# Thresholded attention and a bilinear feed-forward on one core: the key slot shared by two heads is spread over four tiles of the array, and a part of it is added by VectorE

## The chip, the cores and the metric

The kernel runs on one core of a Trainium2 chip. The metric is the device time of one execution in microseconds. Before the change it was 1560.83 us in the median of three runs (1559.9 to 1564.76). One further execution was profiled; it took 1561.63 us, and its instructions span 1559.9 us.

In what follows TensorE is PE in the profile, VectorE is DVE, ScalarE is ACT, GpSimd is POOL, and SyncE, which issues most DMAs, is SP.

## The reference

There are 8 batches, 8 heads, 576 positions and a head dimension of 64. All values are float32.

```python
scores = scale * q @ k.T
thresh = max(scores, axis=-1) - tau
attn = exp(where(scores >= thresh, scores, -1e9) - max)
attn = attn / (sum(attn) + 1e-9)
x = (attn @ v)                 # heads side by side: (4608, 512)
out = ((x @ w_a) * (x @ w_b)) @ w_out      # d_ff = 1536
```

The change touches the line `attn @ v` alone.

## The kernel before, in words

**Pairs and units.** Two heads of a batch form a pair, so there are 32 pairs, four to a batch. A pair's 576 queries are cut into five units: four of 128 queries for each of both heads, and a last one with the 64 remaining queries of both heads. The main loop runs over 160 units, `g` counting them. In the first batch the units are ordered for an early start. From the second batch on, units 0 and 1 of all four pairs of a batch come first, and then units 2, 3 and the last one pair by pair.

**What a unit does.** `scores` (L303) writes the scores of 128 rows into one PSUM tile per head, and the last unit into a single one; the last unit uses only the two tiles on the diagonal of the array. VectorE takes the maxima (`mx`, L319), GpSimd scales them (L320), ScalarE takes the exponential (L332), and VectorE masks by the threshold and sums (`w`, L336). ScalarE normalises (L355). In the next iteration `turn_blocks` (L393) transposes blocks on VectorE and writes them to a scratch in DRAM, from where `turn_back` reads them as `wT`, with keys on the partitions. The first eight units go through TensorE instead. Queries and keys of later pairs are transposed by VectorE too (`prep`, L282, tiles `qT` and `kT`), two and one iterations ahead of their first use.

**The product.** `weighted` (L483) runs three iterations after the last unit of its part, at the end of the iteration but for a fifth of the feed-forward's share. It has 256 query columns, or 320 where the 64 tail queries ride along; in the first batch the tails are products of 64 columns, and the first eight units are products of 128 in `weighted_unit` (L469). `product` (L441) uses the array as four tiles of 64 by 64. A tile (r, j) reads the 64 partitions of half r and writes those of half j. The 576 keys of two heads fill nine slots of 128 partitions: head 0 has slots 0 to 3, head 1 has slots 5 to 8, and slot 4 (`NT`) holds 64 keys of head 0 in its lower half and 64 keys of head 1 in its upper half. So in slots other than 4 all four tiles work, two on each head, and in slot 4 only tiles (0, 0) and (1, 1). The two halves of the key rows of a head go into two banks, `pv[:, 0]` and `pv[:, 1]`, and `join` (L437) adds them: ScalarE copies the first into `xT` and VectorE adds the second. For 320 columns a second `join` does the same for the tail, into `xt`.

**The feed-forward** works in blocks of 256 tokens. Its matmuls (`pab` and `po`, L530 and L550) are a generator that `advance` steps by as many columns as the iteration is owed. When the four pairs of a block are done, GpSimd copies `xT` with its partition halves exchanged into `xS` (L459), and the block is queued.

**What sets the order.** The order of the instructions on every engine is the order in which the program writes them; `keep_order` ties each to the one before. All PSUM tiles come from one pool of four buffers of two banks each: scores, `pab`, `po` and `pv` take turns, and a matmul that opens a tile waits until the last reader of an earlier one is done. `make_room` (L596) moves the feed-forward into the middle of a `pab` or `po` before a product takes its tile.

Of the kernel before, what the change touches and what calls it, by code (L numbers as in the profile page):

```python
# [14 lines left out]
ALU = mybir.AluOpType  # L15
# [35 lines left out]
def kernel(  # L51
# [36 lines left out]
    nc = tc.nc  # L88
    B, H, S, D = q.shape
    P = 128  # L90
    Q = 32
# [3 lines left out]
    NT = 4  # L95
    MAIN = NT * P
    TAIL = S - MAIN
# [7 lines left out]
    GT = HALF // TAIL  # L105
# [16 lines left out]
    def banks(n, name):  # L122

        return psum.tile([P, 2, 512], FP32, tag="banks", name=name)[:, :, 0:n]
# [43 lines left out]
    for f in range(NG):  # L168
        for c in range(HP):
            for dst, w in ((wa_sb, w_a), (wb_sb, w_b)):  # L170
                src = []
                for r in range(2):
                    chunks = [(2 * c + e) % HP * 2 + (r + (c >= HP // 2)) % 2 for e in range(2)]
                    cols = slice(f * CW + r * CH, f * CW + (r + 1) * CH)
                    rows = w[:, cols].bitcast(U32).rearrange("(k p) f -> p k f", p=D)
# [69 lines left out]
    for _ in range(2):  # L245
        t = work.tile([P, 2 * NB, 2 * Q], FP32, tag="tb", bufs=2, name="rows")
        t = t.rearrange("p n e -> p (n e)")[0:R]
# [11 lines left out]
    for name in ("q", "k"):  # L259
        t = work.tile([P, CW, 2], FP32, tag="xT", bufs=XT_BUFS, name="rows")  # L260
        t = t.rearrange("p n e -> p (n e)")[0:R, 0:2 * NR * D]
# [17 lines left out]
    x_of, xtail_of = {}, {}  # L279
# [110 lines left out]
    def width(i, h):  # L390
        return (HALF, HALF, TAIL)[h] if i < HP else (HALF, HALF + TAIL)[h]
# [45 lines left out]
    def join(out, lo, hi):  # L437
        nc.scalar.copy(out, lo)  # L438
        nc.vector.tensor_tensor(out, out, hi, op=ALU.add)  # L439

    def product(wT, vm, n):  # L441

        pv = banks(n, "pv")
        for s in (NT, 0, 1, 2, 3):
            for r in range(2):
                rows = slice(r * D, (r + 1) * D)
                for j in ((r,) if s == NT else range(2)):
                    k0 = NT if s == NT else 5 * j + s
                    nc.tensor.matmul(pv[j * D:(j + 1) * D, r], vm[rows, k0], wT[rows, k0],  # L449
                                     start=(s == (NT if j == r else 0)), stop=(s == NT - 1))  # L450
        return pv

    def x_tile(name):
        return work.tile([P, HP, HALF], FP32, tag="xT", bufs=XT_BUFS, name=name)
# [14 lines left out]
    def weighted_unit(i, u):  # L469

        b, hp = pairs[i]
        pv = product(turned.pop((i, u, "pe")), loaded[i]["v"], P)
        if (b, 0) not in x_of:
            x_of[b, 0] = x_tile("xT")
            state["xs"] = x_tile("xS")
        join(x_of[b, 0][:, hp, u * P:(u + 1) * P], pv[:, 0], pv[:, 1])
        exchange(x_of[b, 0], state["xs"], hp, u * P, (u + 1) * P, nc.vector)
        if hp == HP - 1:
            state["rows"] = u + 1
            if u == 0:  # L480
                blocks.append(((x_of[b, 0], state["xs"]), ("first", b, 0)))

    def weighted(i, h):  # L483

        b, hp = pairs[i]
        n = width(i, h)
        pv = product(turned.pop((i, h)), loaded[i]["v"], n)
        if h < 2:
            if hp == 0:
                x_of[b, h] = x_tile("xT")  # L490
            lo, hi = (pv[:, r, 0:HALF].rearrange("p (i t e) -> p i t e", t=2, e=Q) for r in range(2))
            join(x_of[b, h][:, hp, :].rearrange("p (t i e) -> p i t e", t=2, e=Q), lo, hi)
            if hp == HP - 1:
                complete.append((x_of.pop((b, h)), ("half", b, h)))
        if n % HALF:
            t = b % GT
            if hp == 0 and t == 0:
                xtail_of[b // GT] = x_tile("xt")
            join(xtail_of[b // GT][:, hp, t * TAIL:(t + 1) * TAIL], pv[:, 0, n - TAIL:n], pv[:, 1, n - TAIL:n])
            del loaded[i], prepared[i]  # L500
            if hp == HP - 1 and t == GT - 1:
                complete.append((xtail_of.pop(b // GT), ("tail", b - t, 0)))
# [120 lines left out]
    n = 0  # L623
# [8 lines left out]
    for g in range(len(units) + PV_LAG):  # L632
# [5 lines left out]
        if here:  # L638
            i, u = units[g]
# [60 lines left out]
        n = g - PV_LAG  # L700
        if BY_PE <= n < len(units) and part(*units[n]):
            make_room()
            weighted(*part(*units[n]))
            running["owed"] -= (NSLOT + 1) // 2 * width(*part(*units[n]))
# [38 lines left out]
```

## Time and profile before

| | |
|---|---|
| median of three runs | 1560.83 us |
| profiled execution | 1561.63 us, span 1559.9 us |
| mean granted TensorE clock | 0.985 |
| TensorE, matmuls | 1490.9 us busy, 22640 records |
| VectorE | 881.9 us, 1844 |
| ScalarE | 592.7 us, 935 |
| GpSimd | 260.3 us, 662 |
| HBM | 127.40 MB read, 89.65 MB written |

A group line gives the source line, the engine, the operation, out<-in by tile names, the shapes and the count; then the busy time in us and the mean of one in ns; then the idle time of the engine just before such instructions and what ended most of it. A line of the timeline gives start in us, length in us, engine, source line, operation and count. A line of the chain gives start, length and what it was. A window line gives, after the stretch and its length, busy us of PE, weight loads, DVE, ACT and POOL with counts, then the granted clock, the share of the DMA engines and GB/s. A float32 matmul leaves two records, one for each of its two passes.

### The profile page before, as it was taken

To read this page: it belongs to the slowest core of one execution; us is meant where nothing else is said; L and a number is where in the kernel's file an instruction comes from. 1 tells how busy PE (TensorE), PEld (TensorE's weight loads), DVE (VectorE), ACT (ScalarE), POOL (GpSimd) and SP (SyncE) were. 2 spreads that over 40 slices of the span, in tenths; PEclk is the share of its full clock that TensorE was granted. 3 is DMA by queue.
4 is the path that set the end of the run, shared out by engine and by line. 5 is a ranking of instruction groups with operands and counts; after the bars stand their busy time and mean duration, and the time that the engine had idled before them with its cause. 6 is when DMAs were issued, how large, how long until landed. Compare 5 with 4: busy or idle time off the path is not lost.

```text
span 1559.9 us, 51105 instructions
## 1 busy us (share of the span) xinstructions
PE 1490.9 (96%) x22640; PEld 1087.8 (70%) x22640; DVE 881.9 (57%) x1844; ACT 592.7 (38%) x935; POOL 260.3 (17%) x662
## 2 busy tenths in 40 slices
PE   5779999898999999999999999999999999999998
PEld 3666585674768777677867686867686768586775
DVE  5999576465656665675544755466555765510010
ACT  4767344343434443443332443243433443310000
POOL 2666211111111111121100101011110111010000
PEclk8889999998999999999999999999999999999999
DMA  9648887679767886687455965588657976530000
GB/s 202 147 139 225 179 159 166 141 151 193 158 141 169 175 194 142 157 171 179 101 128 117 187 151 140 114 174 180 150 130 140 186 160 140 130 85 16 2 15 15
DMA packets 624558, 220.38 MB, mean 141 GB/s; under 512 B 542929, under 2 KB 612049, under 8 KB 624337
## 3 DMA queue, kind: packets, MB, share of 16 engines
q1 hardware_dynamic: 621968, 216.52, 63.4%
q8 instruction: 178, 2.92, 0.8%
q10 hardware_dynamic: 2368, 0.59, 0.2%
q14 instruction: 44, 0.35, 0.1%
HBM read 127.40 MB, written 89.65 MB: 139 GB/s over the span
## 4 chain that ended last, share of the span: by engine, by line
PE 77%; DVE 8%; DMA 5%; SPq 3%; ACT 2%; issue 2%; POOL 0%; DVEq 0%; POOLq 0%; ACTq 0%
PE pab L530 42%; PE po L550 19%; PE pv L449 8%; PE sc L312 8%; SPq L411 2%; DVE w L336 2%; DMA wT<-swap 2%; DVE mx L319 2%; DMA swap<-tb 2%; DVE low L226 1%; DVE tb L401 1%; SPq L140 1%; DMA qm<-in_q_dram 1%; SPq L423 0%; DMA raw<-in_moe_w_b_dram 0%
## 5 line engine op out<-in xcount | busy, mean ns | idle before, releaser
L550 PE MATMUL po<-wo_sb,h 64*64 64x512 f32 x3456 | 410.1, 590 | 0.0
L332 ACT ACTIVATE w<-sc,bias,scalars 128x576 f32<-128x576 f32 x288 | 228.6, 829 | 237.1 <-POOL bias L320 233.8
L550 PEld LDWEIGHTS po<-wo_sb,h 64*64 64x64 f32 x3456 | 178.8, 133 | 178.9 <-issue 166.5
L319 DVE TENSOR_REDUCE mx<-sc 128x1 f32<-128x576 f32 x288 | 205.8, 751 | 163.8 <-PE sc L312 160.1
L355 ACT ACTIVATE w<-w,rcp 128x576 f32<-128x576 f32 x272 | 197.7, 769 | 234.5 <-DVE rcp L349 234.5
L320 POOL TENSOR_SCALAR bias<-mx,scalars 128x1 f32<-128x1 f32 x288 | 84.8, 294 | 1073.5 <-DVE mx L319 1042.9
L530 PE MATMUL pab<-xS,wa_sb 64*64 64x256 f32 (+1 forms) x3520 | 260.2, 377 | 2.4 <-POOL xS L459 2.4
L312 PE MATMUL sc<-kT,qT 64*64 64x288 f32 x2304 | 239.6, 412 | 21.4 <-DVE kT L301 8.1
L530 PE MATMUL pab<-xS,wb_sb 64*64 64x256 f32 (+1 forms) x3520 | 257.3, 375 | 0.0
L336 DVE SCALAR_TENSOR_TENSOR w<-sc,thr,w 128x576 f32<-128x576 f32 x288 | 222.6, 805 | 18.0 <-ACT w L332 13.8
L530 PE MATMUL pab<-xT,wb_sb 64*64 64x256 f32 (+1 forms) x3136 | 224.2, 378 | 3.2 <-DVE h L538 1.6
L530 PE MATMUL pab<-xT,wa_sb 64*64 64x256 f32 (+1 forms) x3136 | 221.8, 373 | 4.9 <-DVE xT L439 3.5
L530 PEld LDWEIGHTS pab<-xS,wa_sb 64*64 64x64 f32 x3520 | 182.2, 134 | 34.9 <-POOL xS L459 9.0
L530 PEld LDWEIGHTS pab<-xS,wb_sb 64*64 64x64 f32 x3520 | 183.7, 134 | 27.2 <-issue 0.3
L449 PE MATMUL pv<-wT,vm 64*64 64x320 f32 (+3 forms) x2592 | 180.4, 389 | 13.9 <-DMA wT<-swap 13.2
L312 PEld LDWEIGHTS sc<-kT,qT 64*64 64x64 f32 x2304 | 137.5, 134 | 71.7 <-issue 26.2
L530 PEld LDWEIGHTS pab<-xT,wa_sb 64*64 64x64 f32 x3136 | 158.6, 133 | 33.0 <-DVE xT L439 3.8
L530 PEld LDWEIGHTS pab<-xT,wb_sb 64*64 64x64 f32 x3136 | 160.4, 136 | 30.4 <-DVE h L538 2.6
L449 PEld LDWEIGHTS pv<-wT,vm 64*64 64x64 f32 x2592 | 129.8, 136 | 59.9 <-issue 24.5
L401 DVE STREAM_TRANSPOSE tb<-w 128x576 f32<-128x576 f32 x240 | 171.2, 751 | 0.0
L538 DVE TENSOR_TENSOR h<-h,pab 128x512 f32<-128x512 f32 (+1 forms) x110 | 72.6, 660 | 139.3 <-PE pab L530 135.7
L439 DVE TENSOR_TENSOR xT<-xT,pv 128x256 f32<-128x256 f32 (+1 forms) x68 | 27.5, 404 | 208.2 <-ACT xT L438 208.2
(59 smaller groups left out, 769.5 us busy)
## 6 DMA issues: line engine op xcount, KB each, us to landing
swap<-tb SPq DMA_DIRECT2D x240, 288.0 KB, 5.1
wT<-swap SPq DMA_DIRECT2D x28, 1440.0 KB, 7.6
wT<-swap SPq DMA_DIRECT2D x32, 1152.0 KB, 6.2
vm<-in_v_dram SPq DMA_DIRECT2D x32, 288.0 KB, 4.2
swap<-tbt SPq DMA_DIRECT2D x128, 72.0 KB, 2.5
out_dram<-osb SPq DMA_DIRECT2D x32, 256.0 KB, 3.8
qm<-in_q_dram SPq DMA_DIRECT2D x112, 72.0 KB, 3.5
km<-in_k_dram SPq DMA_DIRECT2D x112, 72.0 KB, 4.8
```

Of the source, the lines that this page charges most:

```text
L312: nc.tensor.matmul(sc[j if u < NT else 0][to, c], qT[r, q0:q0 + D], kT[r, c * SH:(c + 1) * SH], start=True, stop=True)
L319: nc.vector.tensor_reduce(mx[:, c], sc[j], axis=AX.XY, op=ALU.max)
L320: nc.gpsimd.tensor_scalar(bias[:, c], mx[:, c], e_nscale, None, op0=ALU.mult)
L332: nc.scalar.activation(w.rearrange("p (c k) -> p c k", c=2), s, AF.Exp, bias=bias[:, j:j + 1], scale=e_scale)
L336: nc.vector.scalar_tensor_tensor(out=wv, in0=s, scalar=thr[:, j:j + 1], in1=wv, op0=ALU.is_ge, op1=ALU.mult, accum_out=sums[:, j:j + 1])
L355: nc.scalar.activation(w, w, AF.Copy, scale=rcp[:, j:j + 1])
L401: nc.vector.transpose(tb[:, j * NB:(j + 1) * NB, (u % 2) * Q:(u % 2 + 1) * Q], w.rearrange("p (n e) -> p n e", e=Q))
L411: nc.sync.dma_start(swap[:, :, g * 2 * Q:(g + 1) * 2 * Q].rearrange("c p w -> p c w"), tb[g * Q:(g + 1) * Q])
L449: nc.tensor.matmul(pv[j * D:(j + 1) * D, r], vm[rows, k0], wT[rows, k0], start=(s == (NT if j == r else 0)), stop=(s == NT - 1))
L530: nc.tensor.matmul(pab[c * D:(c + 1) * D, r], w[rows, f // n, k, fs + c * D:fs + (c + 1) * D], moving, start=(k == 0), stop=(k == H - 1))
L538: nc.vector.tensor_tensor(ht, ht, pab, op=ALU.mult)
L550: nc.tensor.matmul(po[c * D:(c + 1) * D, r], ht[rows, t0:t0 + D], wo_sb[rows, F, :], start=(F == 0), stop=(F == NF - 1))
```

## The change

In `product` slot 4 comes last instead of first. Its diagonal tiles compute only the first 128 columns (`m`). The other columns, 128 of 256 or 192 of 320, are computed by the two tiles off the diagonal, from the same keys and weights, into further columns `n` to `2 n - m` of the same banks. There they stand in the other partition half than the one they belong to. So after each `join` VectorE adds them to `xT`, 64 partitions at a time, in two adds of 128 columns that read the one half and write the other, and for 320 columns in two more of 64 columns to `xt`. Products of 64 and of 128 columns have no such rest; in them only the order changes.

```diff
     def product(wT, vm, n):
-        pv = banks(n, "pv")
-        for s in (NT, 0, 1, 2, 3):
+        m = min(n, P)
+        pv = banks(2 * n - m, "pv")
+        for s in (0, 1, 2, 3, NT):
             for r in range(2):
                 rows = slice(r * D, (r + 1) * D)
-                for j in ((r,) if s == NT else range(2)):
-                    k0 = NT if s == NT else 5 * j + s
-                    nc.tensor.matmul(pv[j * D:(j + 1) * D, r], vm[rows, k0], wT[rows, k0],
-                                     start=(s == (NT if j == r else 0)), stop=(s == NT - 1))
+                for j in range(2):
+                    cols = slice(j * D, (j + 1) * D)
+                    if s < NT:
+                        nc.tensor.matmul(pv[cols, r, 0:n], vm[rows, 5 * j + s], wT[rows, 5 * j + s],
+                                         start=(s == 0), stop=(s == NT - 1 and j != r))
+                    elif j == r:
+                        nc.tensor.matmul(pv[cols, r, 0:m], vm[rows, NT], wT[rows, NT, 0:m],
+                                         start=False, stop=True)
+                    elif n > m:
+                        nc.tensor.matmul(pv[cols, r, n:2 * n - m], vm[rows, NT], wT[rows, NT, m:n],
+                                         start=True, stop=True)
...
-            join(x_of[b, h][:, hp, :].rearrange("p (t i e) -> p i t e", t=2, e=Q), lo, hi)
+            x = x_of[b, h][:, hp, :].rearrange("p (t i e) -> p i t e", t=2, e=Q)
+            join(x, lo, hi)
+            for r in range(2):
+                to, of = (slice(c * D, (c + 1) * D) for c in (r, 1 - r))
+                more = pv[of, r, n:n + P].rearrange("p (i t e) -> p i t e", t=2, e=Q)
+                nc.vector.tensor_tensor(x[to, 2:4], x[to, 2:4], more, op=ALU.add)
...
-            join(xtail_of[b // GT][:, hp, t * TAIL:(t + 1) * TAIL], pv[:, 0, n - TAIL:n], pv[:, 1, n - TAIL:n])
+            x = xtail_of[b // GT][:, hp, t * TAIL:(t + 1) * TAIL]
+            join(x, pv[:, 0, n - TAIL:n], pv[:, 1, n - TAIL:n])
+            for r in range(2 if n > TAIL else 0):
+                to, of = (slice(c * D, (c + 1) * D) for c in (r, 1 - r))
+                nc.vector.tensor_tensor(x[to], x[to], pv[of, r, n + P:n + P + TAIL], op=ALU.add)
```

## The prediction

> **What bounds the kernel now.** I read the page first, then the granted clock, then one window over the steady part, then the groups with shapes kept apart, and last the timeline and the chain around single products. The page and the window:
>
> ```profile
> span 1559.9 us, 51105 instructions
> PE 1490.9 (96%) x22640; PEld 1087.8 (70%) x22640; DVE 881.9 (57%) x1844; ACT 592.7 (38%) x935; POOL 260.3 (17%) x662
> ...
> 390.00:1400.00 1010.00, 1003.99 (x15408) 744.97 (x15404) 593.54 (x1280) 390.32 (x588) 134.78 (x436) 1.00 0.69 151
> ```
>
> TensorE is busy for 1004.0 of 1010.0 us at full clock there, VectorE (third figure) for 59%. So the time is TensorE's, and VectorE seems to have room. Whether it has room at the place of the change is another question. The groups concerned:
>
> ```profile
> L449 PE MATMUL pv<-wT,vm 64*64 64x320 f32 x1008 | 85.7, 442 | 6.4 <-DMA wT<-swap 6.4
> L449 PE MATMUL pv<-wT,vm 64*64 64x256 f32 x1152 | 78.2, 385 | 6.9 <-DMA wT<-swap 6.8
> L439 DVE TENSOR_TENSOR xT<-xT,pv 128x256 f32<-128x256 f32 x60 | 25.3, 421 | 207.8 <-ACT xT L438 207.8
> L439 DVE TENSOR_TENSOR xt<-xt,pv 128x64 f32<-128x64 f32 x32 | 7.1, 221 | 18.7 <-ACT xt L438 18.7
> L439 DVE TENSOR_TENSOR xT<-xT,pv 128x128 f32<-128x128 f32 x8 | 2.2, 273 | 0.3 <-ACT xT L438 0.3
> ```
>
> A product has 18 matmuls and each leaves two records, so 1152/36 = 32 products have 256 columns and 1008/36 = 28 have 320. One of 256 on TensorE's timeline:
>
> ```profile
> 709.00 2.15 PE L449 MATMUL pv<-wT,vm 64*64 64x256 f32 x34
> 710.79 0.41 PE L312 MATMUL sc<-kT,qT 64*64 64x288 f32 x2
> 710.95 0.42 PE L449 MATMUL pv<-wT,vm 64*64 64x256 f32 x2
> ```
>
> The scores start at 710.79 on the tiles that the shared slot leaves idle, while the product still runs on the other two until 711.16. So the idle tiles are not idle for long, they run ahead; the two tiles on the diagonal set the pace, with ten passes in 2.16 us: 216 ns for 256 columns, 0.844 ns a column (the 320-column passes lie 270 ns apart, the 128-column ones 108).
>
> What follows a product, on the chain that ended last:
>
> ```profile
> 693.14 0.38 ACT xT L438
> 693.54 0.43 DVE xT L439
> 694.00 0.22 ACT xt L438
> 694.25 0.07 DVE xt L439
> 694.38 1.41 DVE mx L319 x2
> 695.80 0.71 DVE tb L401 x2
> 697.77 0.82 DVE w L336 x3
> 698.59 0.69 DVE kT L286
> 699.43 0.42 PE sc L312
> ```
>
> For 6.3 us the end of the kernel hangs on ScalarE and VectorE in order, and TensorE's next scores wait for kT. The change inserts VectorE work in the middle of this.
>
> [...] the two mx reductions overlap by 0.08 us, while the half-partition copies to the other half (L459 on VectorE, first phase) start 0.034 us after the add they need, follow each other 0.014 us apart, and the next instruction comes 0.032 us later. [...] the trace has 273 for 128 and 221 for 64, on 128 partitions, and I use these.
>
> **The change, part by part.** *Removed on TensorE.* A diagonal tile's slot pass shrinks to 128 columns, twice per product: (256-128) x 2 x 0.844 = 216 ns, and (320-128) x 2 x 0.844 = 324 ns. The other two tiles of a 320 product get 192 columns each, 108 ns more than the diagonal; I cost this at nothing because the half-idle last score unit (diagonal only) just before it puts them about 0.4 us ahead. Without that cover it is 28 x 0.108 = 3.0 us. Sum: 32 x 0.216 + 28 x 0.324 = 6.9 + 9.1 = **16.0 us**. Moving the slot from first to last place costs the diagonal nothing; products of 64 and 128 columns change in order only. No DMA is added or moved.
>
> *Added on VectorE.* 32 x 2 + 28 x 4 = 176 adds, about 45 us of busy time. As busy time it would be free. As delay, D: after the join, 0.034 + 0.273 + 0.014 + 0.273 = 0.59 us[...]. For 256 columns mx waits 0.13 us for its scores anyway, so D is 0.49. For 320, ScalarE's copy of xt today waits for VectorE's join of xT (0.03 us after it), so I take it to wait for the two adds too; then the join of xt, two more adds (0.034 + 0.221 + 0.014 + 0.221 = 0.49), and mx, which overlapped by 0.08, is held 0.03: D = 0.59 + 0.49 + 0.11 = 1.2. Bounds for D(320): 0.9 if the copy of xt does not wait for the adds, 1.5 if the adds take the 344 ns that the half-partition copies average. Queued behind on VectorE are both mx, the transposes, the masking with sums (w), and kT; behind ScalarE's xt copy, the next exponentials.
>
> *Who waits.* TensorE's next scores or pab need the PSUM banks that w or the pv joins free, or kT. I took, after each product, the start of the waiting matmul less the end of its VectorE release, less the 0.15 us that such a release takes at least; this is the spare. VectorE's idle time comes only after these waits, so nothing else absorbs D. A matmul may wait with no idle time shown, since a tile still runs: at 653.19 the second score bank waits for w, ended 653.04, while the page counts no gap.
>
> 28 products of 320 columns, by the end of their join: no spare at 310.8, 334.2, 515.7, 538.6, 649.4, 672.8, 694.5, 885.3, 1037.4, 1060.7, 1207.6, 1229.7 (five wait for kT, seven for w); part at 355.8 (0.88), 469.9 (0.66), 492.8 (0.27), 804.7, 834.5, 1155.1, 1323.2 (0.76 each), 860.8 (0.54), 1351.2 (0.46); above 1.2 at the other seven. Loss: 12 x 1.2 = 14.4, plus the nine shortfalls to 1.2, 5.0 us.
> 32 products of 256: no spare at 141.5 (w, and mx does not wait: 0.6), 235.7, 400.8 and 553.8 (kT, 0.49 each): 2.1. Three whole blocks (187, 284, 383 us) start when GpSimd has exchanged x, and it starts after the adds: 3 x 0.59 = 1.8.
> Four or five products start when wT lands (182, 277, 374, 566): a faster product before them gains nothing, about 1.0.
>
> **Sum.** -16.0 + 14.4 + 5.0 + 2.1 + 1.8 + 1.0 = **+8.3 us**. The profiled execution took 1561.63 us with a span of 1559.9; I expect a span near 1568, and against the median of 1560.83 a time of **1569**.
>
> **Rivals.** *Adds hidden (faster).* VectorE is 41% idle in the steady part and idles 3 to 5 us ahead of most joins. Then only the 1 us at the DMAs is lost: -15, 1546. Against it: the chain above, where no TensorE work lies between the joins and the scores.
> *Only waits with visible idle time count (faster to same).* If TensorE makes up the waits that show no gap, because other tiles run on, then kT (5 x 1.2 + 2 x 0.49 = 7.0), the blocks (1.8) and the DMAs (1.0) are left: -6, 1555. For it: full tiles are busy at most of the w waits. Against: the matmuls are issued in order, and at 653.19 all three other tiles start together, late.
> *Slower evacuation than priced.* D(320) of 1.5 and D(256) of 0.8: 12 x 0.3 + 9 x 0.3 + 7 x 0.3 = 8 more, and the lost lead on the narrow tiles 3 more: +19, 1580. It decides once an add exceeds some 0.34 us.
> *It does not do what it says*, the diagonal keeping its pace because the shorter passes are bound by weight loads (133 ns each against 108 of streaming): the early 128-column products do run at 108 ns a pass, so I give it almost nothing; it would be 16 us worse, 1585.
>
> **From cases to numbers.** Mine 0.5 (its own range 1562 to 1577), adds hidden 0.12, visible waits only 0.2, slower adds 0.15, no gain 0.03. What a measurement here can tell from no change is 0.3%, 4.7 us: below 1556.1 is faster, above 1565.5 slower. Adds hidden and half of the visible case are faster: 0.22. The other half and a fifth of mine are the same: 0.2. The rest is slower: 0.58. The range 1552 to 1581 leaves out the hidden case below and a few of the worst above.
>
> **What would show it.** Right: 128-column forms of pv on all four tiles, products of 1.94 and about 2.4 us instead of 2.16 and 2.70 on the diagonal; VectorE busy 925 to 930 us; the adds near 0.27 and 0.22 us; ScalarE's xt copy waiting about 1.1 us for VectorE instead of 0.49; more time in TensorE's waits for kT and w, 1.5 to 2.7 us at the five kT places; the chain with more VectorE than 8%. Wrong: kT and w waits as long as before (adds hidden), adds much over 0.3 us, or the pv passes unchanged in spacing.

## The result, and the profile after

The changed kernel takes **1575.13 us** in the median (1572.78 to 1577.66), the kernel before 1561.64 us in the runs beside it (1559.9 to 1564.76). The medians differ by 13.5 us. The ratio is 1.0084, with a 95% interval of 1.0059 to 1.011: slower by 9 to 17 us, 13.1 in the middle. The profiled execution took 1576.81 us and spans 1575.0. The prediction said 1569, in a range of 1552 to 1581, with a chance of 0.58 on slower.

The page of the changed kernel (the span, the busy times, the chain by engine), and the same steady stretch that was shown of before:

```profile
span 1575.0 us, 51790 instructions
PE 1487.7 (94%) x22880; PEld 1109.0 (70%) x22880; DVE 935.6 (59%) x2020; ACT 592.0 (38%) x935; POOL 261.4 (17%) x662
PE 75%; DVE 11%; SPq 5%; DMA 4%; ACT 2%; issue 2%; POOL 0%; DVEq 0%; POOLq 0%; ACTq 0%
...
390.00:1400.00 1010.00, 990.91 (x15406) 756.29 (x15402) 640.35 (x1429) 391.98 (x589) 135.46 (x437) 1.00 0.70 152
```

TensorE, the first figure of the window, was busy for 1004.0 of these 1010 us and is busy for 990.9 now. It has less to do and waits longer. VectorE has gone from 593.5 to 640.4 us there, and its share of the chain from 8% to 11%. By busy time nothing is full: VectorE stands at 63% of this stretch.

The groups of the changed kernel with shapes kept apart (L458 is the diagonal of slot 4, L461 the two other tiles, L509 and L520 the adds):

```profile
L458 PE MATMUL pv<-wT,vm 64*64 64x128 f32 x272 | 34.7, 276 | 0.0
L461 PE MATMUL pv<-wT,vm 64*64 64x192 f32 x112 | 14.2, 329 | 0.0
L509 DVE TENSOR_TENSOR xT<-xT,pv 64x128 f32<-64x128 f32 x120 | 34.4, 287 | 2.9
L520 DVE TENSOR_TENSOR xt<-xt,pv 64x64 f32<-64x64 f32 x56 | 12.3, 220 | 1.3
```

The shared slot is spread as meant: the tiles off the diagonal take 192 columns in the products of 320 (56 matmuls of two records each), and the diagonal 128. The adds cost 287 and 220 ns, 46.7 us in all. VectorE's busy time grows by 53.7 us on the page. Added up one by one, its instructions take 48.6 us more (980.7 before, 1029.3 after); the other 5.1 us are overlap between neighbours that is gone, such as that of the join of `xt` with the first maxima (0.08 us at 649 us before, where now 0.03 us pass between the last add and the maxima).

A product of 256 columns on the changed kernel's timeline:

```profile
744.18 1.94 PE L455 MATMUL pv<-wT,vm 64*64 64x256 f32 x32
...
746.07 0.27 PE L458 MATMUL pv<-wT,vm 64*64 64x128 f32 x1
746.13 1.18 PE L312 MATMUL sc<-kT,qT 64*64 64x288 f32 x16
```

From its first start to its last end it takes 746.34 - 744.18 = 2.16 us; the one shown of before took 711.37 - 709.00 = 2.37. (The prediction counted ten passes at their pace, 2.16 before and 1.94 after, and so had the product of before end at 711.16.) The 0.21 us are there. The scores now start 0.2 us before the product's end instead of 0.6: the two idle tiles, which had run ahead into them, no longer do.

What follows a product of 320, on the changed kernel's chain, at a place like the one shown of before:

```profile
1072.47 0.38 ACT xT L438
...
1073.33 0.29 DVE xT L509
...
1073.63 0.29 DVE xT L509
...
1073.95 0.22 ACT xt L438
...
1074.93 1.42 DVE mx L319 x2
...
1079.27 0.70 DVE kT L286
...
1080.10 1.72 PE sc L312 x16
```

From the copy to the maxima it was 694.38 - 693.14 = 1.24 us; now it is 1074.93 - 1072.47 = 2.46. So one product of 320 puts VectorE **1.22 us** later. ScalarE's copy of `xt` starts 0.03 us after the second add ends. The next scores still wait for `kT` at the end of it all.

TensorE's waits between 390 and 1420 us (what it waited for, then us in total, times, longest us), before:

```profile
PE sc L312 <- DVE sums L347: 4.4, 5, 1.5
PE pv L449 <- DMA wT<-swap: 1.0, 3, 0.6
PE sc L312 <- DVE kT L286: 0.6, 1, 0.6
```

and the longest after:

```profile
PE sc L312 <- DVE kT L286: 12.7, 6, 2.9
PE sc L312 <- DVE w L336: 2.7, 5, 0.7
PE pab L551 <- POOL xS L471: 2.4, 1, 2.4
```

The waits that the first list puts down to `sums` are waits for `kT`, which VectorE finishes just before (on the chain shown of before, 0.06 us of `sums` come between `kT` and the scores, in a piece not shown). The same six waits for `kT` grow from 5.0 to 12.7 us, by 1.28 in the mean, and waits for `w` appear, with one of 0.6 under `sums` in a line not shown. The wait for the exchanged `xS` is not new: it stands at 393 us, and in the kernel before at 383, just outside this stretch, with 1.2 us.

### The profile page after: what moved, and what is told of

Same layout as the page of the kernel before. It is cut to its first block, busy times and chain, and to the rows that moved or that the text cites. A ratio compares the mean times of both kernels' runs of the same rounds, so it can differ in the third digit from the quotient of the medians.

```text
span 1575.0 us, 51790 instructions
## 1 busy us (share of the span) xinstructions
PE 1487.7 (94%) x22880; PEld 1109.0 (70%) x22880; DVE 935.6 (59%) x2020; ACT 592.0 (38%) x935; POOL 261.4 (17%) x662
## 4 chain that ended last, share of the span: by engine, by line
PE 75%; DVE 11%; SPq 5%; DMA 4%; ACT 2%; issue 2%; POOL 0%; DVEq 0%; POOLq 0%; ACTq 0%
PE pab L551 39%; PE po L571 20%; PE sc L312 8%; PE pv L455 6%; DVE mx L319 3%; SPq L411 2%; DVE w L336 2%; DVE tb L401 2%; DVE low L226 1%; DMA swap<-tb 1%; SPq L140 1%; DMA qm<-in_q_dram 1%; SPq L423 1%; PE pv L458 1%; DMA km<-in_k_dram 0%
## 5 line engine op out<-in xcount | busy, mean ns | idle before, releaser
L571 PE MATMUL po<-wo_sb,h 64*64 64x512 f32 x3456 | 400.8, 590 | 0.1
L571 PEld LDWEIGHTS po<-wo_sb,h 64*64 64x64 f32 x3456 | 192.9, 133 | 161.0 <-issue 131.6
L312 PE MATMUL sc<-kT,qT 64*64 64x288 f32 x2304 | 222.5, 417 | 33.6 <-DVE kT L286 12.7
L551 PE MATMUL pab<-xS,wa_sb 64*64 64x256 f32 (+1 forms) x3520 | 246.4, 376 | 4.7 <-POOL xS L471 4.7
L551 PE MATMUL pab<-xS,wb_sb 64*64 64x256 f32 (+1 forms) x3520 | 244.1, 375 | 0.0
L336 DVE SCALAR_TENSOR_TENSOR w<-sc,thr,w 128x576 f32<-128x576 f32 x288 | 222.6, 805 | 15.8 <-ACT w L332 13.5
L551 PE MATMUL pab<-xT,wa_sb 64*64 64x256 f32 (+1 forms) x3136 | 214.6, 376 | 4.4 <-DVE xT L439 1.8
L551 PE MATMUL pab<-xT,wb_sb 64*64 64x256 f32 (+1 forms) x3136 | 214.8, 376 | 3.4 <-ACT h L557 1.7
L312 PEld LDWEIGHTS sc<-kT,qT 64*64 64x64 f32 x2304 | 125.6, 136 | 84.1 <-issue 45.8
L455 PE MATMUL pv<-wT,vm 64*64 64x256 f32 (+3 forms) x2304 | 163.8, 391 | 15.5 <-DMA wT<-swap 9.3
L455 PEld LDWEIGHTS pv<-wT,vm 64*64 64x64 f32 x2304 | 115.6, 140 | 51.3 <-issue 27.7
```

The source lines that it names most:

```text
L312: nc.tensor.matmul(sc[j if u < NT else 0][to, c], qT[r, q0:q0 + D], kT[r, c * SH:(c + 1) * SH], start=True, stop=True)
L336: nc.vector.scalar_tensor_tensor(out=wv, in0=s, scalar=thr[:, j:j + 1], in1=wv, op0=ALU.is_ge, op1=ALU.mult, accum_out=sums[:, j:j + 1])
L455: nc.tensor.matmul(pv[cols, r, 0:n], vm[rows, 5 * j + s], wT[rows, 5 * j + s], start=(s == 0), stop=(s == NT - 1 and j != r))
L551: nc.tensor.matmul(pab[c * D:(c + 1) * D, r], w[rows, f // n, k, fs + c * D:fs + (c + 1) * D], moving, start=(k == 0), stop=(k == H - 1))
L571: nc.tensor.matmul(po[c * D:(c + 1) * D, r], ht[rows, t0:t0 + D], wo_sb[rows, F, :], start=(F == 0), stop=(F == NF - 1))
```

## The experiments

Theory A is the prediction's: TensorE gains on each product, and the adds put VectorE's chain later by 1.2 us (0.5 for 256 columns), which is paid in full where the next wait has no spare. The rivals asked whether the order of the slots costs, whether the loss comes from something other than VectorE's time (a PSUM tile that is held longer), and whether the gain on TensorE arrives at all. Times are medians, each with its ratio to the kernel before on the same chip.

**Order alone.** The kernel before with the shared slot last.

```diff
-        for s in (NT, 0, 1, 2, 3):
+        for s in (0, 1, 2, 3, NT):
...
-                                     start=(s == (NT if j == r else 0)), stop=(s == NT - 1))
+                                     start=(s == 0), stop=(s == (NT if j == r else NT - 1)))
```

> The kernel before with one edit: the shared slot comes last in the product instead of first; nothing is spread and nothing is added. Theory A (the change pays on TensorE's diagonal and loses on VectorE's chain): the order costs nothing, within 3 us of the kernel before. Theory B (a part of the 13 us, the 3 us that the changed kernel already has at 140 us, comes from the order): 3 us or more over it.

1562.11 us, ratio 1.0004 (0.9995 to 1.0013). The order costs nothing that can be measured.

**The spread without the adds.** The changed kernel without both adds.

```diff
-                nc.vector.tensor_tensor(x[to, 2:4], x[to, 2:4], more, op=ALU.add)
+                pass
...
-                nc.vector.tensor_tensor(x[to], x[to], pv[of, r, n + P:n + P + TAIL], op=ALU.add)
+                pass
```

> The changed kernel without VectorE's adds; the other columns of the shared slot are computed but never added to the result, so the output lacks that part. Theory A: only the gain on the diagonal is left, 16 us less about 1 us at the waits for transfers, so 15 us under the kernel before (1546 to 1547). Theory C (the shorter passes gain less, because the narrow tiles with 192 columns or the weight loads set the pace): under 10 us of gain.

1548.56 us, ratio 0.9927 (0.99 to 0.9954): 12.6 us faster. So TensorE's gain is real, but of the 16.0 us worked out only about 12.6 arrive. Against before, the starts of ScalarE's copies drift by -0.21 us with each product of 256 and -0.32 with each of 320, with jumps back where a product has to wait for `wT`, where a block starts in the first 400 us, and once at 1225 us (1.0). There a faster TensorE only waits longer:

```profile
PE sc L312 <- DVE sums L347: 4.5, 5, 1.5
PE pv L455 <- ACT w L355: 1.4, 1, 1.4
PE pv L455 <- DMA wT<-swap: 1.3, 1, 1.3
```

These are the longest of its waits from 390 to 1420 us. The `kT` waits are about as long as before (5.3 us with a line of 0.8 not shown, 5.0 before); the 2.7 us at the products were 1.0 before.

**The adds without the spread.** The kernel before with the same 176 adds in the same places, reading columns that the joins have read already.

```diff
-            join(x_of[b, h][:, hp, :].rearrange("p (t i e) -> p i t e", t=2, e=Q), lo, hi)
+            x = x_of[b, h][:, hp, :].rearrange("p (t i e) -> p i t e", t=2, e=Q)
+            join(x, lo, hi)
+            for r in range(2):
+                to, of = (slice(c * D, (c + 1) * D) for c in (r, 1 - r))
+                more = pv[of, r, P:2 * P].rearrange("p (i t e) -> p i t e", t=2, e=Q)
+                nc.vector.tensor_tensor(x[to, 2:4], x[to, 2:4], more, op=ALU.add)
...
+            for r in range(2 if n > TAIL else 0):
+                to, of = (slice(c * D, (c + 1) * D) for c in (r, 1 - r))
+                nc.vector.tensor_tensor(x[to], x[to], pv[of, r, n - TAIL:n], op=ALU.add)
```

> The kernel before, its product untouched, with adds of the same number, size and place after each join; they read the product's own columns of the other half, so the output has a part too much. Theory A: the whole loss without the gain, 23 us by the sum of the prediction and up to 28 by the changed kernel, so 1584 to 1589. Theory D (only waits with visible idle time count): about 10 us over the kernel before.

1588.13 us, ratio 1.0189 (1.0157 to 1.022): 27.0 us slower. Its waits from 390 to 1420 us for `kT` are those of the changed kernel (12.7) almost to the tenth:

```profile
PE sc L312 <- DVE kT L286: 12.6, 6, 2.8
```

The two halves add up: -12.6 + 27.0 = +14.4, within the interval of the whole change. The sum is not sharp: by the ratios the halves are -11 and +30 us, each with 4 to 5 us of uncertainty. So the adds alone bring more than the whole loss. The run does not tell VectorE's time from a `pv` tile that is held longer, since the adds do both.

**Only the products of 256 spread.** The 28 products of 320 stay whole, with the shared slot last.

```diff
-        m = min(n, P)
+        m = P if n == HALF else n
...
-            for r in range(2):
+            for r in range(2 if n == HALF else 0):
...
-            for r in range(2 if n > TAIL else 0):
+            for r in range(0):
```

> The changed kernel with the spread in the 32 products of 256 columns alone; those of 320 keep the shared slot on the diagonal, and have no adds. Theory A: gain 6.9, loss 2.1 at four places without spare and 1.2 where two blocks start, and up to 1 at transfers: 2 to 4 us under the kernel before. Theory E (each product loses alike, whatever its spare): 32 of 60 products keep half the loss, so some 6 us over it.

1561.97 us, ratio 1.001 (1.0001 to 1.0018). A miss: instead of a gain of 2 to 4 us there is none. By the starts of ScalarE's copies the kernel is 5.4 us behind before at 415 us, and from there gains 3.5 us to the end, 0.21 or so per product but for two jumps back of some 0.5 us, at 568 and 1245 us. So something costs far more in the first 400 us than the prediction allowed, though only eight of the 32 products lie there.

**Only the late products of 256 spread.** To test that: the spread and the adds in the 24 products of 256 from the third batch on.

```diff
-        m = min(n, P)
+        m = P if spread else n
...
+        spread = n == HALF and i >= 2 * HP
+        pv = product(turned.pop((i, h)), loaded[i]["v"], n, spread)
...
-            for r in range(2):
+            for r in range(2 if spread else 0):
...
-            for r in range(2 if n > TAIL else 0):
+            for r in range(0):
```

> Spread and adds in the 24 products of 256 columns from the third batch on alone (after about 390 us); all others keep the shared slot on the diagonal. Theory G (the products of 256 lose where transfers of wT or the starts of blocks are awaited, which is in the first 400 us; later they run in VectorE's spare time): gain 5.2, loss 1 to 2, so 3 to 4 us under the kernel before. Theory E (each product loses about what it gains, wherever it is): no difference from the kernel before.

1557.74 us, ratio 0.9977 (0.9968 to 0.9986): 3.6 us faster, of 24 x 0.216 = 5.2. The same edit that gives nothing over the whole kernel gains when the first two batches are left alone. By the starts of ScalarE's copies the two runs end 6.5 us apart; 4.4 of that is there by 415 us. So most of the loss of the run before it, though not all, lies in the first 400 us.

**Another way out of PSUM.** ScalarE copies the rest of the shared slot to the other partition half in SBUF, in two copies per product, and GpSimd adds it one iteration later. VectorE is left as before. No run here has GpSimd read PSUM itself.

```diff
+    def add_rests():
+        while rests:
+            for out, rest in rests.pop(0):
+                nc.gpsimd.tensor_tensor(out, out, rest, op=ALU.add)
+
     def exchange_blocks():
+        add_rests()
...
+        if n > P:
+            rest = work.tile([P, DM], FP32, tag="osb", bufs=OSB_BUFS, name="rest")[:, 0:n - P]
+            for r in range(2):
+                to, of = (slice(c * D, (c + 1) * D) for c in (r, 1 - r))
+                nc.scalar.copy(rest[to], pv[of, r, n:2 * n - P])
...
```

> The changed kernel's matmuls, but the other columns leave PSUM by two ScalarE copies into SBUF, already in the right half, and GpSimd adds them to x one iteration later; VectorE has no adds. The pv tile is held longer than in the kernel before, by two copies of 192 columns or 0.6 to 0.7 us. Theory A (the loss is delay of what queues behind the adds on VectorE): the 12.6 us gain of the run without adds, less 2 to 4 us at block starts and tile waits, so 1550 to 1553. Theory H (the loss is that pv gives its PSUM tile back later, whoever reads it): over half of the 27 us loss stays, so 1563 or more.

1551.74 us, ratio 0.9923 (0.9898 to 0.9949): 11 us faster than before by the medians and 12 by the ratio, as good as without any adds. The timeline of a product of 320 in this kernel:

```profile
646.38 0.22 DVE L439 TENSOR_TENSOR xt<-xt,pv 128x64 f32<-128x64 f32 x1 [0.28 <-ACT xt L438]
646.52 1.42 DVE L319 TENSOR_REDUCE mx<-sc 128x1 f32<-128x576 f32 x2
646.63 0.64 ACT L533 COPY rest<-pv 64x192 f32<-64x192 f32 x2 [0.29 <-DVE xt L439]
...
647.76 1.55 ACT L332 ACTIVATE w<-sc,bias,scalars 128x576 f32<-128x576 f32 x2 [0.49 <-POOL bias L320]
```

VectorE goes from the join to the maxima at once. ScalarE's two copies fall into time in which it waited for the maxima anyway. The tile is still held until 647.27, 0.67 us after the join of `xt`, and that costs nothing that shows. In the changed kernel the adds hold it for 1.1 us longer than before (from the first copy to the last read 2.43 us at 659 us, 1.32 before). So holding the tile does not lose the time, as far as these 0.67 us test it; the place of the adds in VectorE's order does.

**Keys and queries prepared one iteration earlier, in the changed kernel.** If `kT` waits are paid because `kT` stands at the end of the delayed chain, moving its transposes (and their loads) one iteration ahead must return part of the loss.

```diff
-            for name, d in (("q", 2), ("k", 1)):
+            for name, d in (("q", 3), ("k", 2)):
...
-            for name, d in (("q", 4), ("k", 3)):
+            for name, d in (("q", 5), ("k", 4)):
```

> The changed kernel with VectorE's transposes of queries and keys, and their loads, one iteration earlier, so that no scores wait for a kT just made. Theory A: TensorE's 13 us of waits for kT shrink to the waits for w behind them; 5 to 9 us under the changed kernel, 1566 to 1570. Theory F (another wait takes over in full, the place does not matter): within 2 us of the changed kernel.

1566.57 us, ratio 1.0029 (1.0018 to 1.0039). Against the changed kernel's 1.0084 that is 0.55%, 8.6 us, back. No visible wait for `kT` is left from 390 to 1420 us; the whole list of the profiled execution, which with 1560.96 us was the fastest of the twenty, is:

```profile
PE sc L312 <- DVE w L336: 6.8, 9, 1.4
```

**The same in the kernel before.** The control: how much of this has nothing to do with the adds.

> The kernel before with the same shift of the transposes and loads. Theory A: its waits for kT with visible idle time, 5 us, go for the most part; 2 to 5 us under the kernel before, less than the shift brings the changed kernel. Theory F: no change.

1556.86 us, ratio 0.9965 (0.9952 to 0.9978), 5.5 us faster. The `kT` waits of before (5.0 us) were worth that much; its trace shows no wait of TensorE from 390 to 1420 us. That leaves about 3 us of the 8.6 as a return of what the adds had made longer, which is less than the uncertainty of the ratios (4 to 5 us together). What is clear is that with the same shift, on the same chip, the changed kernel stays 10 us slower than the kernel before, and that its waits are then for `w`.

**Both.** The copies on ScalarE, the adds on GpSimd, and the earlier preparation.

> Both: the rest through ScalarE and GpSimd, and the transposes one iteration earlier. Theory A: the gains of both add up to about 11 to 15 us under the kernel before, 1546 to 1550.

1550.34 us, ratio 0.9916 (0.989 to 0.9942). It has the lowest median of the kernels that compute the whole output, and beats both the kernel before and the changed one. From the run without the earlier preparation it can't be told apart, so the two gains (12 and 5.5 us) are not seen to add up.

**Each add twice.** The changed kernel with every add line written twice, so the delay is about doubled.

```diff
                 nc.vector.tensor_tensor(x[to, 2:4], x[to, 2:4], more, op=ALU.add)
+                nc.vector.tensor_tensor(x[to, 2:4], x[to, 2:4], more, op=ALU.add)
...
                 nc.vector.tensor_tensor(x[to], x[to], pv[of, r, n + P:n + P + TAIL], op=ALU.add)
+                nc.vector.tensor_tensor(x[to], x[to], pv[of, r, n + P:n + P + TAIL], op=ALU.add)
```

> The changed kernel with every add made twice, so the rest counts twice in the output. Theory A with the spare counted per product: another 1.1 us of delay for 320 columns and 0.6 for 256; the first delay has used up the spare of 21 products of 320, so the second falls on TensorE nearly in full there (21 x 1.1 = 23), and 3 to 7 more come from the others: 26 to 30 us over the changed kernel, as much as or more than the first set of adds cost in 60 products. Theory I (TensorE catches up, or the delay falls into VectorE's idle time): under 15 us over it.

1617.25 us, ratio 1.0354 (1.0332 to 1.0375): 55 us over before and some 42 over the change, where 26 to 30 were expected. The direction is A's, the size is a miss. Two windows around one of its waits for `kT` (granted clock third from the end) show what was not thought of:

```profile
564.00:567.00 3.00, 0.96 (x16) 0.74 (x20) 2.30 (x7) 0.63 (x1) 2.27 (x6) 0.95 1.03 328
567.00:570.00 3.00, 3.00 (x24) 1.24 (x20) 2.34 (x4) 1.88 (x4) 0.84 (x3) 0.50 1.33 171
```

TensorE works for 0.96 us of the first three, and then runs at half clock (0.50). In this kernel the waits for `kT` come to 19.1 us, the longest 4.0, against 12.7 and 2.9 in the changed one. The mean granted clock is 0.974 in the profiled execution against 0.981 in that of the changed kernel, and 0.974 to 0.978 against 0.980 to 0.986 over the four runs of each. By the spans of the profiled executions that is 42.0 us of clock lost against 29.9; the 12 us between them, less what falls into waits, are an estimate of what closes most of the gap between 42 and 26 to 30. At both places shown, this one and the one of the changed kernel below, the half clock comes after the wait. The run with the earlier preparation agrees: it is the changed kernel without the long waits (1.4 us at most from 390 us on), and its profiled execution has a mean granted clock of 0.986.

## Why the prediction was right, and where it was off

Right were the direction and the mechanism. The size was short: the sum said +8.3 us. The medians differ by 13.5, and in the profiled executions the changed kernel is 15.1 us longer, 3.2 of them in the first 140 us, where only the order of slots differs. These 3.2 are scatter of the start: the kernel before with earlier preparation has them too (3.3 at 140 us) with the old order of slots, and the run with only the products of 256 spread does not, with the new one. From there on the traces give +11.9 us: the gain of 16.0, and losses of 27.9 where the prediction had 24.3. The run with the adds alone measures 27.0 (without the gain that is lost at waits).

The losses by place come from the starts of ScalarE's copy of `xT`, after less before, from one product to the next, with the product's gain added back:

| losses, us | predicted | measured |
|---|---|---|
| twelve products of 320 without spare | 14.4 | 17.0, of it 1.7 half clock |
| their mean, without that | 1.2 | 1.27 |
| products with 0.27, 0.46, 0.54, 0.66 of spare | 0.93, 0.74, 0.66, 0.54 | 0.91, 0.62, 0.64, 0.47 |
| four with 0.76 of spare | 0.44 each | about 0.15 each |
| all from 144 to 400 us | 6.4 | 9.2 |
| all from 400 us on | 17.9 | 18.7 |

That the total from 400 us on agrees within 0.8 us is in part luck: the 1.7 us of half clock were not priced, and the four products with 0.76 of spare were priced 1.2 us too high. Of the two products of 256 without spare there, one pays 0.86 us (at 400 us) and one nothing (at 553 us), where 0.49 each was predicted.

The 6.4 are 1.1 for two products of 256, 2.7 for three of 320, 1.8 for the blocks and 0.8 of the 1.0 at transfers.

- **Gain per product** (216 and 324 ns): right, 0.21 and 0.32 at every place that doesn't wait. That products of 320 show the full 0.32 also confirms that the 192 columns of the other two tiles cost nothing that shows.
- **D(320) = 1.2 us**: right, 1.22 on the chain. The estimate had left open whether ScalarE's copy of `xt` waits for the adds. It does:

```profile
L438 ACT COPY xt<-pv 128x64 f32<-128x64 f32 x32 | 6.8, 213 | 32.2 <-DVE xT L509 31.1 <-PE pv L458 1.0
```

31.1 us over 28 products is 1.11 each, against 13.6 / 28 = 0.49 before. The adds of 128 columns were taken as 273 ns and are 287; those of 64 as 221, and are 220. On the chain 0.03 us pass before the first add, 0.01 between the two, and 0.03 between the last add to `xt` and the maxima; the prediction counted 0.034, 0.014 and 0.03.
- **The no-spare products**: the places were right, all twelve paid. Mis-sized by 0.07 each, and at one place by half clock on top.
- **The step that failed most**: "a faster product before them gains nothing, about 1.0". It counts the gain that is lost where a product waits for `wT`, and puts at nothing that the adds delay `wT` itself, whose way (VectorE's transposes, the writing to the scratch, the reading back) begins behind them in VectorE's order. TensorE's waits from 130 to 400 us, two lines of before and three of after:

```profile
PE pv L449 <- DMA wT<-swap: 12.2, 3, 6.2
PE pab L530 <- POOL xS L459: 2.4, 3, 1.2
```

```profile
PE pv L455 <- DMA wT<-swap: 9.0, 2, 7.7
PE pv L455 <- DVE rcp L349: 6.1, 1, 6.1
PE pab L551 <- POOL xS L471: 4.7, 3, 2.4
```

The 6.1 us put down to VectorE's `rcp` stand ahead of the same product that waited for `wT` before. So the waits at these products go from 12.2 to 15.1 us, 2.9 more where 0.8 was predicted. In the run without the adds they are 13.2, so 1.0 is the lost gain, as predicted, and 1.9 come from the adds. The waits of the three block starts for `xS` grow by 0.55, 0.53 and 1.25 us, 2.3 in all where 1.8 was predicted. Together this is 2.6 of the 2.8 us by which the losses before 400 us exceed their price. With only the products of 256 spread, the waits at the products are 16.1 us and those for `xS` 2.6, so there too it is the transfers. These are single executions, one of each kernel. Half clock is no part of it: from 120 to 400 us TensorE works at half clock for 14.6 us before and 15.0 after.
- **The waits named ahead**: 1.5 to 2.7 us at the five `kT` places; measured 12.7 us in six, 2.1 in the mean, from 1.4 to 2.9. The chain's VectorE share rose as said. VectorE's busy time came out at 935.6, not 925 to 930, since overlap between neighbours went with it.

**The rivals.** Adds hidden (1546): fallen, the adds alone cost 27.0 us. Only waits with visible idle time (1555): fallen, twelve of twelve no-spare places pay, seven of which wait for `w` with little or no gap shown. Slower adds (1580): the total came nearest to it on the high side, but its cause isn't there: the adds are at 287 ns, below the 340 from which it decides. No gain (1585): fallen with the run without adds.

**What came on top.** After 400 us the changed kernel runs at half clock once, at the place where the chain shown above waits for `kT`:

```profile
1076.00:1080.00 4.00, 1.25 (x22) 0.79 (x13) 3.97 (x9) 1.56 (x2) 3.29 (x10) 1.00 0.86 146
1080.00:1084.00 4.00, 3.90 (x40) 2.90 (x44) 3.11 (x7) 2.32 (x4) 1.42 (x5) 0.58 0.89 269
```

After 2.85 us without a matmul the scores take 1.72 us instead of 1.20, and the clock is back from 1084 us on (1.00 before the wait, 0.99 in the next 4 us). TensorE is busy for all of the 3.41 us at half clock, so 1.7 us of work are lost. The prediction priced a wait by its own length only.

Not every such wait brings this on here. In the traces of before and after, the stretches of full and of half clock between the first and the last are all whole multiples of 3.41 us. The wait that ends at 1080.10 lies in one such step, from 1077.25 to 1080.66, in which TensorE is busy for 0.56 us, and the next step is at half clock. A wait of the same 2.85 us, for `kT` as well, ends at 904.48; it is divided between two steps, in which TensorE is busy for 55% and 61%, and the clock stays full. The profiled execution with the adds alone has a mean granted clock of 0.982 against 0.985 before, which is 28.5 us of clock lost in the span against 23.4, so by this estimate up to 5 us of its loss, the first 400 us included, are of this kind; the kernel before has no half clock from 400 us until the work is done.

## What to carry to other kernels

An edit that shortens the busiest engine and lengthens another is priced place by place: gain per instance on the one side, and on the other the delay times the number of places where the next wait has no spare; the other engine's busy share (57% here) says nothing about it. If the added work has to be done, put it on the engine that is waiting at that very point: the same sums, copied by ScalarE and added by GpSimd, turned +13 us into -12 (by the ratios). And work that others wait for at the end of such a chain, here `kT`, belongs an iteration earlier, before anything is added ahead of it.

## What the runs showed of the hardware

- A wait of TensorE can cost more than itself: in the changed kernel, after 2.85 us without a matmul, it ran at half clock for 3.41 us, from 1080.66 to 1084.07. In the kernel with the doubled adds it was busy for 0.96 us between 564 and 567 us, and the granted clock was 0.50 in the next 3 us. Of the six waits for `kT` in the changed kernel, 1.4 to 2.9 us long, only the one did it.
- The tiles of the array that had nothing to do at the end of the product started what came next: the scores began about 0.6 us before the end of the product before and 0.2 us after the change. Filling these tiles gained only what it took from the busiest tile (0.21 us of the 2.37).
